# One VectorE step for a complex product, TensorE transposes at the start, and a new order of steps in an attention and convolution kernel

## The chip, the cores and the metric

The kernel runs on one core of a Trainium2 chip. The core has five engines that run side by side and wait for one another through semaphores: TensorE (PE, matrix products), VectorE (DVE), ScalarE (ACT), GpSimd (POOL) and SyncE (SP, which here issues DMAs only). Each engine carries out its own instructions strictly in the order in which they were written. Matrix products land in PSUM, eight banks of 128 x 512 fp32, and are carried ("evicted") from there to SBUF by VectorE or ScalarE; POOL cannot reach PSUM. The metric is the device time of one execution in microseconds (us), the median of several runs; lower is better.

## What is computed

Eight batches, eight heads, 576 positions, 64 features per head. A linear attention with exponential features gives `x`, and a gated long convolution follows, whose convolution is done with a Fourier transform over the 576 positions:

```python
def phi(x):
    proj = np.einsum('bhsd,df->bhsf', x, w_phi)          # 64 -> 128 features
    proj = proj - np.max(np.abs(proj), axis=-1, keepdims=True)
    return np.concatenate([np.exp(proj), np.exp(-proj)], axis=-1)
q_p, k_p = phi(q), phi(k)
kv = np.einsum('bhsf,bhsd->bhfd', k_p, v)
z = np.sum(k_p, axis=2)
x = einsum(q_p, kv) / (einsum(q_p, z) + 1e-6)            # per head, heads side by side: 576 x 512

x1, x2, x3 = split(x @ w_proj, 3)                        # 512 each
X2 = np.fft.rfft(x2, axis=0); H = np.fft.rfft(filter_fft, axis=0)
y = x1 * np.fft.irfft(X2 * H, axis=0) * x3               # X2 * H is the complex product
out = y @ w_out
```

All inputs and the output are fp32 in DRAM; the kernel works in bf16 with fp32 sums.

## The kernel before

**Steps.** Every piece of work is a method of one class, named in a few letters, and most methods issue one instruction or one short group on one engine. They are best read along the path of a batch `b`:

- `load`, `loadh` (L497, L503): POOL issues DMAs that bring a batch of q, k or v (or half of one) to SBUF as bf16. `trh` (L513) is a transposing DMA on SP for half a batch of q or k, from `qn` to `qT`, from `kn` to `kT`.
- `Qn`, `Pk` and `Qnt`, `Pkt` (L535, L528, L542): TensorE projects q and k; `maxq`, `maxk` (VectorE, L600) reduce the absolute maxima from PSUM; `ex`, `exkt`, `exqt` (ScalarE, L584 to L594) write the exponentials. The maxima of q go as two bf16 parts (`mhi`, `mlo`) through a transposing DMA (`trm`, L629, from `mh` to `mT`) back into the q projection (`Pq`, L555), which subtracts them. Those of k scale v: `em` (ScalarE, L634) and `vs` (POOL, L639), one each for both signs and both halves of the heads.
- `KV` (L645) forms kv and z, `KVe` evicts them, `NE` (L669) multiplies by q, `rc` and `xn` (VectorE) divide, and `trx`, `trxt` (L714, L719) are transposing DMAs on SP from `xn` to `xT`.
- `fold`, `foldt` (POOL, L727, L734) form sums and differences of position pairs, `X2` (TensorE, L741) projects them, `X2e` evicts, and `F` (L750, with `dft`, L415) multiplies with DFT tables `fwd`, `fwd5`. `F` has five parts of 128 rows: parts 0 and 1 are a real and an imaginary part, so are 2 and 3, and part 4 has the frequencies left over.
- The complex product with the filter's spectrum: VectorE's `m1` (L756) multiplies each part in PSUM by a table `A`, `Fe` (L753) copies parts 0 to 3 to `C`, POOL's `m2` (L760) multiplies the partner part in `C` by a table `B`, and `m3` (L765) adds.
- `I` (L817) is the inverse transform, even and odd half in two neighbouring banks; `Ie` copies the even half to `es`, `Ip` and `Im` (VectorE, L828) add and subtract. `X1`, `X3` project the gates, `X1e` evicts x1, `tm` multiplies by x3, `ym` (L840) multiplies the gates into the convolution, `O` (L850) projects, `Oe` evicts, and `st` (L860, SP) stores.

A last piece of 64 positions is done apart in most stages (the names with a `t` at the end).

**Set-up.** The DFT tables are made on the chip: POOL counts (`gen_rows`), VectorE and ScalarE form angles and sines into tiles `G` and `g3`, POOL masks some into `G5` (`gen_five`, L367), and two transposing DMAs (`gen_fwd`, `gen_fwd5`, L378) make `fwd` and `fwd5`. POOL also makes `sel` (a one-hot table for the maxima) and `inv`. The filter is loaded (`filt_load`, nine DMAs of 64 KB for each half), folded on POOL (`filt_fold`, L406), transformed (`H`, five matmul groups) and scaled into `A` and `B` (`H_ev`). `warm,n` (L275) issues n matmuls on an idle tile whose product nobody reads: 48 in all, 22 of them at the very start. `late` (L245) closes the set-up tiles and places the tiles of the second half of the kernel in the same memory; it ends with a memset of `eo` on POOL.

**Order.** One string, `PLAN` (L24), lists every step of the kernel in order, with its arguments and, behind `@`, its first PSUM bank; `run` (L874) goes through it word by word. As each engine runs in order, the string sets the order on all five engines and on both DMA queues (SP's and POOL's). Steps of up to three batches are mixed: while attention works on batch b, the second half works on b-1 and stores b-2. A ring (`RING`, L20) gives the number of buffers of each tile; a step takes the buffer `i % n`.

Of the kernel before, what the change touches and what calls it, by code (L numbers as in the profile page):

```python
# [19 lines left out]
RING = {'Ekp': 4, 'Ekm': 4, 'Eqp': 3, 'Eqm': 3, 'vp': 3, 'vm': 3, 'r': 4, 'o': 3, 'kn': 2, 'qn': 2, 'vn': 2, 'kT': 2, 'mk': 2, 'mq': 2, 'mh': 2, 'mT': 2, 'xT': 2, 'xTt': 2, 'KVs': 2, 'Fkp': 2, 'Fkm': 2, 'Fqp': 2, 'Fqm': 2, 'rt': 2, 'xnt': 2, 'xn': 1, 'yT': 2, 'yTp': 2, 'es': 2, 'cv': 2}  # L20
# [16 lines left out]
xn,0,1@0 NE,0,2@0 rc,0,2@0 xn,0,2@0 w_load,proj,2 filt_fold,2 maxkt,1@2 trh,q,1,0 filt_fold,0
filt_fold,1 H,1@4 NE,0,3@0 H_ev,ACT,1@4 rc,0,3@0 rct,0@6 xnt,0,1@6 exkt,m,1@2 xn,0,3@0 H,0@5
trh,q,1,1 xnt,0,0@6 Pk,1,0@2 ex,k,p,1,0@2 trx,0,1 w_load,proj,0 H_ev,DVE,0@5 ex,k,m,1,0@2 gen_inv
trxt,0 Qn,1,0@0 maxq,1,0@0 maxk,1,0@2 trx,0,0 H,2@4 H_ev,ACT,2@4 H,4@6 H_ev,ACT,4@6 warm,4@7  # L40
Pk,1,3@0 Qn,1,1@4 H_fix Qnt,1@6 maxqt,1@6 H,3@2 H_ev,ACT,3@2 X3t,0@3 maxq,1,1@4 load,k,2 em,m,1,0
warm,2@6 Qn,1,3@6 maxq,1,3@6 Qn,1,2@4 ex,k,p,1,3@0 maxq,1,2@4 warm,4@2 Pk,1,2@6 X1t,0@2 maxk,1,2@6
trx,0,3 trx,0,2 X1,0,3@4 late maxk,1,3@0 X1te,ACT,0@2 tmt,0@3 X1,0,2@5 foldt,0,1 mhi,1 w_load,proj,1
em,p,1,0 X1e,DVE,0,2@5 X1,0,0@2 ex,k,p,1,2@6 ex,k,m,1,3@0 X1e,ACT,0,0@2 X1,0,1@3 X1e,ACT,0,1@3
ex,k,m,1,2@6 load,v,1 foldt,0,0 X3,0,2@5 fold,0,0 tm,0,2@5 em,m,1,1 X2,0,4@2 mlo,POOL,1 fold,0,1
X2,0,3@3 X2e,ACT,0,4@2 X2e,DVE,0,3@3 em,p,1,1 X2,0,0@5 X2e,ACT,0,0@5 X3,0,1@2 tm,0,1@2 trm,1
Pq,1,2@6 X1e,DVE,0,3@4 X2,0,1@5 ex,q,p,1,2@6 Pqt,1@2 exqt,p,1@2 X2,0,2@4 trh,k,2,1 X2e,DVE,0,1@5
X2e,DVE,0,2@4 F,0,0@5 X3,0,0@0 exqt,m,1@2 Fe,DVE,0,0@5 tm,0,0@0 ex,q,m,1,2@6 load,q,3 Pq,1,1@2
ex,q,m,1,1@2 ex,q,p,1,1@2 F,0,3@4 m1,0,3@4 m1,0,0@5 F,0,2@0 Fe,DVE,0,2@0 Fe,ACT,0,3@4 F,0,1@1
Fe,DVE,0,1@1 Pq,1,0@6 ex,q,m,1,0@6 load,q,2 load,k,3 vs,m,1,1 vs,p,1,1 KV,1,1@2 KVe,ACT,1,1@2  # L50
vs,m,1,0 m1,0,2@0 vs,p,1,0 trh,k,2,0 KV,1,0@4 KVe,ACT,1,0@4 m2,0,1 m1,0,1@1 m2,0,0 m3,POOL,0,0
NE,1,2@2 rc,1,2@2 xn,1,2@2 m2,0,2 trh,q,2,0 m2,0,3 warm,1@0 NEt,1@4 rct,1@4 xnt,1,1@4 xnt,1,0@4
ex,q,p,1,0@6 Pq,1,3@0 trh,q,2,1 trx,1,2 NE,1,0@6 ex,q,p,1,3@0 ex,q,m,1,3@0 rc,1,0@6 xn,1,0@6
Pk,2,3@2 maxk,2,3@2 F,0,4@4 m1,0,4@4 w_load,out NE,1,1@6 trx,1,0 warm,2@5 NE,1,3@0 rc,1,1@6 xn,1,1@6
ex,k,m,2,3@2 rc,1,3@0 xn,1,3@0 Pk,2,1@4 ex,k,m,2,1@4 m3,POOL,0,1 ex,k,p,2,3@2 trxt,1 Qn,2,0@6
maxq,2,0@6 maxk,2,1@4 I,0,1@0 Ie,0,1@0 Ip,0,1@0 Im,0,1@0 ym,POOL,0,1 I,0,0@6 Ie,0,0@6 Im,0,0@6
Ip,0,0@6 ym,POOL,0,0 ex,k,p,2,1@4 trx,1,3 trx,1,1 Pkt,2@2 exkt,p,2@2 Qn,2,2@0 exkt,m,2@2 maxq,2,2@0
maxkt,2@2 Pk,2,0@4 ex,k,m,2,0@4 Qnt,2@6 maxqt,2@6 Qn,2,1@0 trh,k,3,1 ex,k,p,2,0@4 Qn,2,3@2
maxq,2,1@0 maxq,2,3@2 mhi,2 X3,0,3@6 X1,1,1@7 X1e,ACT,1,1@7 foldt,1,0 maxk,2,0@4 tm,0,3@6 I,0,3@0
Ie,0,3@0 em,m,2,0 Ip,0,3@0 Im,0,3@0 load,v,2 I,0,2@2 Ie,0,2@2 foldt,1,1 X2,1,4@7 Ip,0,2@2 Pk,2,2@4  # L60
fold,1,0 X2,1,0@6 X2e,ACT,1,4@7 X2,1,1@7 mlo,POOL,2 trm,2 em,p,2,0 X1,1,3@0 fold,1,1 ex,k,m,2,2@4
ex,k,p,2,2@4 Im,0,2@2 ym,DVE,0,3 ym,DVE,0,2 X2e,DVE,1,0@6 Pq,2,0@2 ex,q,m,2,0@2 O,0,1@1 Oe,ACT,0,1@1
ex,q,p,2,0@2 maxk,2,2@4 X1,1,2@6 trh,k,3,0 Pq,2,1@4 ex,q,p,2,1@4 X2e,DVE,1,1@7 ex,q,m,2,1@4 load,k,4
X1e,DVE,1,3@0 em,p,2,1 X2,1,2@1 X1e,DVE,1,2@6 st,0,1 Pqt,2@2 exqt,m,2@2 trh,q,3,0 vs,p,2,0 X2,1,3@0
X2e,DVE,1,3@0 vs,m,2,0 X2e,DVE,1,2@1 KV,2,0@6 Pk,3,0@4 KVe,ACT,2,0@6 maxk,3,0@4 F,1,1@0 m1,1,1@0
load,v,3 exqt,p,2@2 em,m,2,1 NE,2,1@6 rc,2,1@6 xn,2,1@6 F,1,4@1 vs,p,2,1 vs,m,2,1 ex,k,p,3,0@4
ex,k,m,3,0@4 Pq,2,2@2 ex,q,p,2,2@2 NE,2,0@6 m1,1,4@1 Pq,2,3@4 ex,q,p,2,3@4 rc,2,0@6 trh,k,4,0
xn,2,0@6 trx,2,0 Fe,DVE,1,1@0 F,1,0@1 m1,1,0@1 KV,2,1@6 m2,1,0 KVe,DVE,2,1@6 F,1,3@0 m1,1,3@0
ex,q,m,2,2@2 NE,2,2@6 rc,2,2@6 Pk,3,1@2 xn,2,2@6 ex,q,m,2,3@4 NE,2,3@4 load,k,5 Fe,ACT,1,0@1 m2,1,1
m3,POOL,1,0 ex,k,p,3,1@2 rc,2,3@4 xn,2,3@4 F,1,2@1 m1,1,2@1 trx,2,1 ex,k,m,3,1@2 trx,2,2  # L70
Fe,ACT,1,2@1 O,0,0@6 Oe,ACT,0,0@6 maxk,3,1@2 Fe,ACT,1,3@0 X3,1,1@7 tm,1,1@7 NEt,2@4 rct,2@4
xnt,2,1@4 X1t,1@1 X1te,ACT,1@1 m2,1,3 xnt,2,0@4 Pk,3,3@2 ex,k,p,3,3@2 maxk,3,3@2 X3,1,3@6 trx,2,3
# [106 lines left out]
class Kernel:  # L179
# [746 lines left out]
```

## Time and profile before

| | us |
|---|---|
| median of 3 runs | 351.43 (348.18 to 353.04) |
| profiled execution, whole time | 351.93 |
| its span, first to last instruction | 350.0 |
| PE busy / PEld busy | 303.4 / 169.5 |
| DVE busy | 257.7 |
| ACT busy | 224.4 |
| POOL busy | 252.3 |
| mean granted TensorE clock | 0.943 of full speed |

The profile is one execution. PE is TensorE's matmuls, PEld its weight loads, which overlap them. A group line reads: line, engine, operation, tile written `<-` tiles read, shape written `<-` shapes read, count, then busy us and mean ns of one, then the idle time of the engine just before them and what ended it. "Idle before" of an engine that doesn't set the time costs nothing. The rows of digits cut the span into 40 slices of 8.75 us: a 9 is a slice that is busy for 90% or more, and in the clock's row a 5 is half speed. A row of the busy times by stretch gives the stretch, its length, the busy time and count of PE, PEld, DVE, ACT and POOL, the granted clock, the DMA engines' mean busy share and GB/s. The timeline and the chain of waits begin with a start time and a duration.

### The profile page before, as it was taken

What the parts mean: (1) busy time and instruction counts of PE and PEld (TensorE: products, weight loads), DVE (VectorE), ACT (ScalarE), POOL (GpSimd) and SP (SyncE); (2) the same over time, 40 slices, a digit from 0 to 9 for tenths busy, and PEclk for the clock granted to TensorE, in tenths of its full rate; (3) what the DMA queues carried; (4) which work ended last, traced back from release to release, by engine and by line L of the source; (5) the groups of instructions that cost most, each with busy time, mean ns of one, the idle gap of its engine ahead of it and who ended that gap; (6) DMA issues with size and microseconds to landing.
All of it is one profiled execution on the core that took longest, in us unless ns stands there. A gap on an engine that the chain in (4) does not pass through costs nothing.

```text
span 350.0 us, 9418 instructions
## 1 busy us (share of the span) xinstructions
PE 303.4 (87%) x3881; PEld 169.5 (48%) x3881; DVE 257.7 (74%) x426; ACT 224.4 (64%) x355; POOL 252.3 (72%) x218
## 2 busy tenths in 40 slices
PE   3560487995979999999998999799999999999982
PEld 1230364443634555556445655454556554665441
DVE  2474048954798789888898898979888987774761
ACT  2746568664667887578477875588567756843531
POOL 8495990889479589898965759456967779678440
PEclk9985559999889999999999999899999999999998
DMA  7999999899979999977495786674695710442236
GB/s 112 154 178 117 173 171 162 137 111 176 148 114 153 128 155 156 185 149 123 83 160 97 98 123 114 106 128 95 137 168 97 109 32 8 101 85 61 53 69 150
DMA packets 83258, 42.68 MB, mean 122 GB/s; under 512 B 63712, under 2 KB 78176, under 8 KB 83216
## 3 DMA queue, kind: packets, MB, share of 16 engines
q1 hardware_dynamic: 68112, 25.25, 45.6%
q0 software_dynamic: 15104, 16.85, 34.0%
q8 instruction: 30, 0.49, 0.6%
q14 instruction: 12, 0.10, 0.1%
HBM read 33.75 MB, written 9.44 MB: 123 GB/s over the span
## 4 chain that ended last, share of the span: by engine, by line
PE 76%; DVE 10%; DMA 8%; ACT 2%; issue 2%; SPq 0%; DVEq 0%; ACTq 0%; POOLq 0%
PE ps L774 17%; PE ps L744 10%; PE ps L427 9%; PE ps L854 8%; PE ps L822 7%; PE ps L656 5%; PE ps L677 4%; DMA mT<-mh 3%; DMA qT<-qn 3%; PE ps L561 3%; DVE yT L842 2%; DVE mq L600 2%; PE ps L540 2%; PE ps L533 2%; PE ps L567 2%
## 5 line engine op out<-in xcount | busy, mean ns | idle before, releaser
L774 PE MATMUL ps<-xT,wproj 128*128 128x512 bf16 x256 | 65.4, 388 | 0.5 <-DVE xnt L708 0.3
L761 POOL TENSOR_TENSOR t<-C,B 128x512 bf16<-128x512 bf16 x32 | 36.4, 1153 | 24.1 <-DVE C L663 21.0
L600 DVE TENSOR_REDUCE mq<-ps 128x8 f32<-128x1024 f32 (+1 forms) x40 | 43.2, 1108 | 9.9 <-PE ps L540 9.5
L600 DVE TENSOR_REDUCE mk<-ps 128x8 f32<-128x1024 f32 (+1 forms) x40 | 43.9, 1110 | 3.6 <-PE ps L533 2.6
L641 POOL TENSOR_TENSOR vp<-vn,vp 128x1152 bf16<-128x1152 bf16 x16 | 34.8, 2177 | 15.9 <-ACT vp L635 15.9
L584 ACT ACTIVATE Eqm<-ps 128x1024 bf16<-128x1024 f32 x32 | 32.6, 1030 | 14.4 <-PE ps L567 13.8
L842 POOL TENSOR_TENSOR yT<-cv,x1s 128x576 bf16<-128x576 f32 x22 | 27.9, 1277 | 18.2 <-DVE cv L831 15.4
L744 PE MATMUL ps<-wproj,eo 128*128 128x512 bf16 x160 | 39.1, 380 | 0.0
L854 PE MATMUL ps<-wout,yT 128*128 128x512 bf16 x144 | 36.2, 380 | 2.0 <-DVE x1s L663 1.0
L427 PE MATMUL ps<-x2n,fwd 128*128 128x512 bf16 x136 | 35.8, 388 | 2.1 <-DVE x1s L663 2.1
L774 PEld LDWEIGHTS <-wproj 128*128 128x128 bf16 x256 | 23.4, 99 | 26.3 <-issue 2.4
L641 POOL TENSOR_TENSOR vm<-vn,vm 128x1152 bf16<-128x1152 bf16 x16 | 34.4, 2151 | 2.2 <-DMA vn<-in_v_dram 1.6
L584 ACT ACTIVATE Ekm<-ps 128x1024 bf16<-128x1024 f32 x32 | 32.7, 1026 | 4.6 <-PE ps L533 3.6
L732 POOL TENSOR_TENSOR eo<-xT 128x1024 bf16<-128x1024 bf16 x16 | 34.0, 2132 | 2.2 <-DMA xT<-xn 2.2
L584 ACT ACTIVATE Eqp<-ps 128x1024 bf16<-128x1024 f32 x32 | 32.5, 1030 | 4.8 <-PE ps L567 2.4
L584 ACT ACTIVATE Ekp<-ps 128x1024 bf16<-128x1024 f32 x32 | 32.7, 1025 | 3.7 <-DVE mk L600 1.8
L661 ACT COPY o<-ps 128x512 f32<-128x512 f32 x29 | 17.0, 587 | 25.6 <-PE ps L854 20.1
L831 DVE TENSOR_TENSOR cv<-es,ps 128x288 f32<-128x288 f32 x64 | 26.1, 447 | 6.6 <-ACT es L826 6.2
L769 POOL TENSOR_TENSOR Y<-Y,t 128x1024 bf16<-128x1024 bf16 x14 | 29.6, 2123 | 1.8 <-DVE Y L757 1.0
L757 DVE TENSOR_TENSOR Y<-ps,A 128x512 bf16<-128x512 f32 x40 | 26.8, 682 | 4.3 <-PE ps L427 4.2
L822 PE MATMUL ps<-inv,Y 128*128 128x288 bf16 x192 | 27.9, 288 | 0.7 <-DVE xn L696 0.4
L811 DVE TENSOR_TENSOR x1s<-ps,x1s 128x512 bf16<-128x512 f32 x32 | 21.8, 686 | 7.6 <-PE ps L774 6.7
(142 smaller groups left out, 635.5 us busy)
## 6 DMA issues: line engine op xcount, KB each, us to landing
out_dram<-o SPq DMA_DIRECT2D x72, 128.0 KB, 2.4
vn<-in_v_dram POOLq DMA_DIRECT2D x8, 576.0 KB, 8.1
kn<-in_k_dram POOLq DMA_DIRECT2D x7, 576.0 KB, 6.7
qn<-in_q_dram POOLq DMA_DIRECT2D x7, 576.0 KB, 8.6
wproj<-in_moe_w_proj_dram POOLq DMA_DIRECT2D x3, 512.0 KB, 6.8
qn<-in_q_dram POOLq DMA_DIRECT2D x2, 288.0 KB, 4.9
kn<-in_k_dram POOLq DMA_DIRECT2D x2, 288.0 KB, 6.5
fl<-in_moe_filter_fft_dram POOLq DMA_DIRECT2D x9, 64.0 KB, 8.6
```

The lines of the kernel that those rows point to most:

```text
L427: self.mm(self.pb(0), l, r, start=(i == 0), stop=(i == len(ks) - 1))
L584: self.nc.scalar.activation(e, self.db(), AF.Exp, bias=0.0, scale=1.0 if g == "p" else -1.0)
L600: self.nc.vector.tensor_reduce(out=out, in_=src, axis=AX.X, op=ALU.max, apply_absolute_value=True)
L641: self.nc.gpsimd.tensor_tensor(out=t[:, :, :, 0:64], in0=self.at("vn", b)[:, 2 * X:2 * X + 2], in1=t[:, :, :, 64:65].to_broadcast([128, 2, ...
L732: self.nc.gpsimd.tensor_tensor(out=o, in0=x[:, :, :, 0, :], in1=x[:, :, :, 1, :], op=op)
L744: self.mm(self.pb(0), eo[:, kt, 128 * c:128 * c + 128], w[:, kt, 512:1024], start=(kt == 0), stop=(kt == 3))
L761: self.nc.gpsimd.tensor_tensor(out=self.at("t2", b)[:, t, :], in0=self.at("C", b)[:, t ^ 1, :], in1=self.at("B")[:, t, :], op=ALU.mult)
L769: e.tensor_tensor(out=Y, in0=Y, in1=self.at("t2", b)[:, s, :], op=ALU.add)
L774: self.mm(self.pb(0), w[:, kt, f0 + 128 * m:f0 + 128 * m + 128], x[:, kt, :], start=(kt == 0), stop=(kt == 3))
L822: self.mm(self.pb(e, 0, 288), Y[:, t, 128 * m:128 * m + 128], inv[:, e, i, :], start=(i == 0), stop=(i == 2))
L842: e.tensor_tensor(out=self.at("yT", b)[:, m, 0:SEQ], in0=self.at("cv", 4 * b + m).rearrange("p j h t -> p (j h t)"), in1=self.at("x1s", b) ...
L854: self.mm(self.pb(0), y[:, kt, 128 * j:128 * j + 128], w[:, kt, :], start=(kt == 0), stop=(kt == 3))
```

## The change

It has three parts.

1. **Complex product.** `Fe`, `m2` and the tiles `C` and `t2` are gone. The filter tables `A` and `B` become one tile `AB` with four pieces for each pair of parts. `m12` reads a part once from PSUM as an operand that is repeated (broadcast) over two pieces of `AB`, and writes both products, 128 x 1024, into a `Y` of four pieces. `m3` adds pieces 0 and 1 to 2 and 3. Part 4 keeps `m1`.
2. **Transposes.** For q and k of batches 0 and 1, for `fwd` and `fwd5`, and for `mT` of batch 0, TensorE transposes 128 x 128 blocks with an identity into PSUM as bf16 (`flip`), up to eight blocks in a bank, and ScalarE or VectorE copies them out (`flop`). The other batches keep the DMA transposes. (`txp`, `txtp` and their copies are defined but not used.)
3. **Order.** `PLAN` is new throughout. `warm` and `hold` do not occur in it. The two halves of `I` are separate steps with a bank each. Buffers of `es`, `cv` and `o` are named in the plan behind `#`. The rings of `Eq` and `v` grow from three to four. The filter loads are all on SP. Twelve evictions of X1 and its tail, seven of O and most of `ym` change their engine, as do ten of `KV`.

```diff
-RING = {... 'Eqp': 3, 'Eqm': 3, 'vp': 3, 'vm': 3, ...}
+RING = {... 'Eqp': 4, 'Eqm': 4, 'vp': 4, 'vm': 4, ...}
+PLACED = ('es', 'cv', 'o')
 PLAN = """
-w_load,phi w_phi zeros loadh,q,0,0 loadh,q,0,1 gen_rows loadh,k,0,0 trh,q,0,0 warm,22@0 Qn,0,0@0
-gen_cols,1 gen_turns,1 gen_cols,0 gen_turns,0 gen_angles,1 Qn,0,1@2 gen_angles,0 maxq,0,0@0
...
+loadh,k,0,0 w_load,phi gen_rows filt_load,SP,1 gen_pads gen_cols,1 loadh,q,0,0 ident gen_cols,0
+gen_turns,1 loadh,q,0,1 loadh,k,0,1 gen_turns,0 gen_angles,1 gen_selidx filt_load,SP,0 zeros
+gen_sin,1 gen_angles,0 gen_five gen_sin,0 tg,0@0 gen_sel tg,2@1 tp,k,0,1@2 tge,DVE,2@1 tp,k,0,0@3
+tpe,ACT,k,0,1@2 tg,1@1 load,k,1 tpe,ACT,k,0,0@3 tp,q,0,1@2 gen_selx tp,q,0,0@4 tpe,ACT,q,0,1@2
+tp,q,0,3@5 tpe,DVE,q,0,0@4 tp,q,0,2@6 w_phi tpe,DVE,q,0,3@5 tpe,ACT,q,0,2@6 tp,k,0,3@7 load,v,0
+tpe,DVE,k,0,3@7 tge,ACT,0@0 Qnt,0@2 Qn,0,0@4 maxqt,0@2 Qn,0,2@6 gen_inv maxq,0,0@4 tp,k,0,2@0
...
+ex,k,p,0,3@4 mlo,DVE,0 Pkt,0@0 filt_fold,2 maxkt,0@0 tpe,ACT,k,1,1@7 Pk,0,2@4 load,q,1 em,p,0,0
+tmp,0@3 maxk,0,2@4 H,0@6 tmpe,ACT,0@3 w_load,proj,0 tpe,ACT,k,1,0@2 exkt,p,0@0 vs,p,0,0 H,3@7
+H_ev,DVE,0@6 em,m,0,0 exkt,m,0@0 em,m,0,1 ex,k,m,0,2@4 Pq,0,1@2 trh,k,2,0 ex,k,p,0,2@4 vs,m,0,0
+H_ev,DVE,3@7 Pqt,0@0 em,p,0,1 ex,q,m,0,1@2 Pq,0,0@4 KV,0,0@6 exqt,m,0@0 vs,p,0,1 ex,q,p,0,1@2
...
@@ H_ev
-            mul(A[:, t, :], acc, s)
-            mul(A[:, t + 1, :], acc, s)
+            mul(AB[:, 0, :], acc, s)
+            mul(AB[:, 3, :], acc, s)
...
-            mul(B[:, t, :], acc, s)
-            mul(B[:, t - 1, :], acc, -s)
+            mul(AB[:, 1, :], acc, s)
+            mul(AB[:, 2, :], acc, -s)
...
+    def pt(self, n):
+        return self.ps[:, self.bank, :].bitcast(BF16)[:, 0:128 * n]
+    def ident(self):
+        idx = self.scr.tile([128, 128], FP32, name="ididx")
+        g = self.nc.gpsimd
+        g.iota(idx, pattern=[[1, 128]], base=0, channel_multiplier=-1,
+               allow_small_or_imprecise_dtypes=True)
+        g.tensor_scalar(out=self.at("idn"), in0=idx, scalar1=0.0, scalar2=None, op0=ALU.is_equal)
+    def flip(self, src, c, n):
+        p, z = self.pt(n), self.at("idn")
+        for i in range(n):
+            self.nc.tensor.transpose(p[:, 128 * i:128 * i + 128],
+                                     src[:, 128 * (c + i):128 * (c + i) + 128], z)
+    def flop(self, eng, dst, n):
+        self.copy(eng, dst, self.pt(n))
+    def tp(self, n, b, i):
+        self.flip(self.at(n + "n", b).rearrange("p v j d -> p (v j d)"), *self.part4(i))
+    def tg(self, i):
+        src = (self.G if i < 2 else self.G5).rearrange("p t x -> p (t x)")
+        self.flip(src, *((0, 8), (8, 4), (0, 5), (5, 5))[i])
+    def tmp(self, b):
+        self.flip(self.at("mh", b).rearrange("p g h x -> p (g h x)"), 0, 1)
...
-    def Fe(self, eng, b, t):
-        self.copy(eng, self.at("C", b)[:, t, :], self.pb(0))
+    def m12(self, b, t):
+        i, h = t // 2, slice(2 * (t % 2), 2 * (t % 2) + 2)
+        self.nc.vector.tensor_tensor(
+            out=self.at("Y", b)[:, i, h, :],
+            in0=self.pb(0).rearrange("p (i x) -> p i x", i=1).to_broadcast([128, 2, 512]),
+            in1=self.at("AB")[:, i, h, :], op=ALU.mult)
     def m1(self, b, t):
-        self.nc.vector.tensor_tensor(out=self.at("Y", b)[:, t, :], in0=self.pb(0), in1=self.at("A")[:, t, :],
+        self.nc.vector.tensor_tensor(out=self.at("Y4", b), in0=self.pb(0), in1=self.at("A4"),
                                      op=ALU.mult)
-    def m2(self, b, t):
-        self.nc.gpsimd.tensor_tensor(out=self.at("t2", b)[:, t, :],
-                                     in0=self.at("C", b)[:, t ^ 1, :],
-                                     in1=self.at("B")[:, t, :], op=ALU.mult)
     def m3(self, eng, b, i):
-        ...
-        e.tensor_tensor(out=Y, in0=Y, in1=self.at("t2", b)[:, s, :], op=ALU.add)
+        Y = self.at("Y", b)[:, i]
+        self.pick(eng).tensor_tensor(out=Y[:, 0:2, :], in0=Y[:, 0:2, :], in1=Y[:, 2:4, :],
+                                     op=ALU.add)
-    def I(self, b, m):
-        Y, inv = self.at("Y", b), self.at("inv")
-        for e in range(2):
-            for i, t in enumerate((2 * e, 2 * e + 1, 4)):
-                self.mm(self.pb(e, 0, 288), Y[:, t, 128 * m:128 * m + 128], inv[:, e, i, :],
-                        start=(i == 0), stop=(i == 2))
+    def I(self, b, m, e):
+        Y, inv, d = self.at("Y", b)[:, e], self.at("inv")[:, e], slice(128 * m, 128 * m + 128)
+        for i, y in enumerate((Y[:, 0, d], Y[:, 1, d], self.at("Y4", b)[:, d])):
+            self.mm(self.pb(0, 0, 288), y, inv[:, i, :], start=(i == 0), stop=(i == 2))
```

From batch 2 on the new order repeats nearly the same sequence of steps for every batch; this is the part from the projection of the maxima of batch 4 to its KV:

```
trh,k,5,1 F,3,0@3 Im,2,2@1#0 em,m,4,0 exkt,m,4@6 Ip,2,2@1#0 F,3,1@0 em,m,4,1 m12,3,2@2
ex,k,m,4,2@4 F,3,4@1 trh,k,6,0 vs,m,4,0 ex,k,p,4,2@4 m12,3,0@3 Pq,4,1@6 em,p,4,1 Pqt,4@4 m12,3,1@0
ex,q,m,4,1@6 F,3,3@2 vs,p,4,1 X3,3,1@3 exqt,m,4@4 m12,3,3@2 ex,q,p,4,1@6 X3,3,0@0 tm,3,1@3
exqt,p,4@4 Pq,4,0@6 vs,m,4,1 m1,3,4@1 KV,4,0@4 ...
```

## The prediction

> **What bounds the kernel now.** I read the page first: busy shares, and the span in 40 slices of 8.75 us.
>
> ```profile
> PE 303.4 (87%) x3881; PEld 169.5 (48%) x3881; DVE 257.7 (74%) x426; ACT 224.4 (64%) x355; POOL 252.3 (72%) x218
> ...
> PE   3560487995979999999998999799999999999982
> ...
> PEclk9985559999889999999999999899999999999998
> ```
>
> TensorE is full from slice 7 on and loses its time in the first seven slices. But 303 us of "busy" counts each matmul's latency. I need its spacing when nothing stands in the way, and take that from the chain of waits, which gives each block with its count.
>
> ```profile
> 5.80 11.05 DMA qT<-qn
> ...
> 26.11 11.31 DMA mT<-mh
> ...
> 70.56 2.59 PE ps L744 x12
> ```
>
> Twelve 512-column matmuls in 2.59 us are 0.216 each. In the same way: 0.122 for 288 columns (L822, twelve in 1.47), 0.016 in KV (L656, 72 in 1.15), 0.031 in NE (L677, 32 in 1.00), some 0.03 for a 128-column projection (starts in the timeline). Counts times spacings: 713 x 0.216 = 154, I 23, KV 18, NE and NEt 20, tails 8, projections 33: 256 us of 350. I also counted the matmuls starting in each stretch at these spacings: 13 us of work in 0 to 60, 47 in 60 to 125, 185 in 125 to 330 (90%), 12 after that. So 94 us are lost: **47 in the head, 18 in the next 65 us, 20 in the long middle, 8 at the end.**
>
> Who holds TensorE in the middle: busy time by stretch (columns: stretch, its length, then PE, PEld, DVE, ACT, POOL with counts, the clock, the DMA share).
>
> ```profile
> 30.00:37.00 7.00, 0.00 (x0) 0.00 (x0) 0.08 (x1) 2.36 (x6) 6.53 (x5) 0.50 1.51 96
> ...
> 45.00:49.00 4.00, 4.00 (x103) 3.58 (x103) 1.33 (x3) 1.57 (x3) 4.00 (x6) 0.50 1.66 202
> ...
> 125.00:300.00 175.00, 170.97 (x2250) 94.42 (x2250) 153.12 (x236) 124.66 (x202) 136.30 (x99) 0.99 0.70 116
> 300.00:330.00 30.00, 30.00 (x351) 17.42 (x344) 20.07 (x40) 15.14 (x27) 21.95 (x17) 1.00 0.30 66
> ```
>
> Where VectorE is 87% busy, TensorE's work fills about 90% of the slots; where VectorE is at 67%, 99%. VectorE's evictions pace TensorE. The first matmuls of KV for batches 0 to 7 start at 41.9, 81.3, 115.9, 147.2, 184.0, 219.8, 259.4 and 298.9: **36.6 us a batch** from batch 2 to 7, and 51 us after the last.
>
> **The product.** Durations by line and shape, and what POOL waited for:
>
> ```profile
> L600 DVE TENSOR_REDUCE mk<-ps 128x8 f32<-128x1024 f32 x32 | 38.6, 1218 | 3.6 <-PE ps L533 2.6 <-ACT Ekp L584 0.9
> ...
> L761 POOL TENSOR_TENSOR t<-C,B 128x512 bf16<-128x512 bf16 x32 | 36.4, 1153 | 24.1 <-DVE C L663 21.0 <-ACT C L661 1.4 <-PE ps L427 1.2
> ...
> L757 DVE TENSOR_TENSOR Y<-ps,A 128x512 bf16<-128x512 f32 x40 | 26.8, 682 | 4.3 <-PE ps L427 4.2
> ...
> L663 DVE CAST C<-ps 128x512 bf16<-128x512 f32 x20 | 13.4, 684 | 4.0 <-PE ps L427 3.9
> ```
>
> Gone are 32 of the 40 multiplies (21.8 us of VectorE), the copies to C (VectorE 13.4, ScalarE 12 x 0.590 = 7.1) and all of m2 (POOL 36.4). New are 32 multiplies of 1024 outputs, whose PSUM operand is read twice; no row shows one. Below: m3 on VectorE, 1024 in 0.694, all from SBUF. Above: ym on VectorE (L842), 576 in 1.432, hence 2.5 for 1024. Nearest is L600, 1024 elements from PSUM in 1.218, in line with 682 ns for 512. I take 1.22: 39.0 us in all, 4 more than what leaves VectorE.
>
> The new order also moves evictions: seven O copies (4.8) and eight X1 copies (5.5) to ScalarE, eight of ten ym (11.5) to POOL, where they cost 8 x 1.277 = 10.2, and ten KV copies (7.0) to VectorE. Back to back, VectorE starts come 0.08 us sooner than durations say (L600 1.13, L757 0.60). At such spacings a batch needs 29.3 us of VectorE before and 28.0 after (15.4 of it maxima, m12 and m1), 31.6 of TensorE both times, some 24 of ScalarE, and of POOL 25 instead of 30.
>
> **The head.** The eight transposing DMAs of batches 0 and 1's q and k go, with the two for the DFT tables and batch 0's mT; the two waits of the chain above (11.05, 11.31) were of that kind. SP gets the nine filter loads that POOL issued (0.5 each). In their place TensorE makes 95 transposes of 128x128, and 21 copies leave PSUM. The nearest row for a transpose is a 128-column projection: 0.03 to 0.06 spacing, 0.22 latency. At 0.06 that is 6 us, beside a TensorE that was idle for 47; at 0.22 it is 21, of which I would expect 10 on the path. The copies hold up to 1024 two-byte elements; by the 256- and 1024-element rows of ScalarE each costs 0.37 to 1.03, some 10 us of ScalarE and 4.5 of VectorE, under the POOL chain that follows.
>
> The Trainium skill, "TensorE: Matmul & The Clock Gate", Part 4, puts a transpose at about 275 ns inside a kernel and says that the full clock doesn't engage for it. By that, 95 x 0.275 = 26 us (an estimate); no row here shows it.
>
> The 48 fillers on idle operands go (15.4 us of latency time). The rows above show what they kept up: despite them the clock stood at 0.50 from 30 to 49. So I charge nothing for their loss before batch 0, and up to 3 us after it. Part 1 of that page has the clock halved after an idle window of about 3.4 us and restored by as long a busy one; by that rule all 9 us of TensorE's early work would take 18, again inside its idle time.
>
> What is late next is **POOL's queue**, in its new order. VectorE no longer begins with the wait for w_phi (4.94 us), so the sines come some 2.5 us sooner, at 11. Then POOL: mask products (L373, L375) 5.1, one-hot 1.5, load of k 0.8, sel 2.1, load of v 0.8, inv 3.5, load of k 0.8: 26. The six filter sums, 6 x 1.268 less overlap: 33. Two loads, 1.6; two scalings of v (L641), 4.3: **KV of batch 0 at 39**, 3 sooner than now. TensorE has H ahead of the q projections, so they also wait for the filter sums at 33.
>
> From there the gap closes further, since now POOL stands still in front of the folds:
>
> ```profile
> 51.52 0.79 POOL L498 DMA_DIRECT2D kn<-in_k_dram  x1
> 62.52 0.31 POOL L261 MEMSET eo<- 128x256 bf16 x1 [10.21 <-issue]
> 62.80 0.42 POOL L738 TENSOR_TENSOR eo<-xTt 128x128 bf16<-128x128 bf16 x1
> ...
> 65.11 2.14 POOL L732 TENSOR_TENSOR eo<-xT 128x1024 bf16<-128x1024 bf16 x1
> ```
>
> The memset (late) follows the last readers of the set-up tiles, the H matmuls. In the new order H,4 comes right after NE of batch 0, at about 50; xn is done at 51, its transposes land 3.7 us later, a fold takes 2.1: **first X2 matmul near 57, against 70.6 now.**
>
> **The sum.** From 57 on TensorE has 242 us of spacing (its 262 less some 20 in the head). Idle: 8 at the end as now; in the middle 200 us of work at 93%, that is 34.0 a batch, 15; 5 while batch 1 fills. 57 + 242 + 28 = 327. The profiled execution is 351.9 for a span of 350.0, so **329 us**. It stands 0.5 us over the median of 351.43 (348.18 to 353.04), which is what the ratio is taken against. About 2% is what this kernel's measurement can tell from no change. I take 93%, between 90 and 99%, because VectorE is lighter by 4% and the folds and m3 no longer wait for 4.6 us of m2 a batch.
>
> **The rivals.**
> - *The order, not the load, sets the period.* By the list of steps, 32.5 us of TensorE's work lie between two KV starts now; the same efficiency over 31.6 makes 35.6 and 340 in all, the upper end of my own case. At 36.5 to 37.5, seven batches cost 2.5 to 3.5 us more each: 346 to 354. For it: both orders are written out, TensorE runs in order, and each attention step needs two of eight banks. If m12 costs 2.5 us, VectorE needs 33 us a batch, at 90% of a period 37, and it comes to the same, near 350. Against: 300 to 330 above, where lighter VectorE meant a full TensorE.
> - *The transposes of xn arrive late: slower.* SP issues two transposes of q for the next batch just before the four of xn; a pair holds SP for up to 6.47 us (timeline at 5.8). By my count X1 of the new batch needs xT about 3 us after it lands. If queueing adds over 7.5 us to the 2.5 us median, every batch loses 4.5, seven of them 31: 360. Against: the DMA share is 0.70 in the middle, and the early transposes are gone from the crowded stretch.
> - *The product's shorter path lets TensorE run at 97 to 99%,* as in 300 to 330: 311 to 318.
> - *The change doesn't do what it says*: TensorE's transposes take longer than the DMAs, by the 0.22 or worse, 10 to 14 us later in the head: 339 to 343.
>
> **Chances.** 0.60 for the forecast (320 to 340), 0.12 for the fast case, 0.06 for slow transposes on TensorE, 0.14 for the order (346 to 354), 0.08 for slower. Range 311 to 347: it leaves out the slow case and the upper part of the order. Faster by over 2% (under 344.4): 0.78; same 0.14; slower 0.08.
>
> **What would show it.** m12 near 1.22 us; KV of batch 0 near 39 with POOL without gaps before it; X2 from 57; KV starts 33 to 35 apart; VectorE under 90% of the middle; about 50 us behind the last KV. I am wrong if POOL idles in the head (then another engine sets it), or if TensorE's matmuls wait for xT or for bank releases by more than 15 us in the middle.

## The result, and the profile after

The changed kernel takes 331.32 us (median of four runs, 329.35 to 332.42) against 352.24 (348.18 to 353.55) for the kernel before: **0.944 of the time, 95% interval 0.933 to 0.954**. The prediction was 329. Run once more beside other kernels it took 327.55, a ratio of 0.941 [0.935, 0.947]. The profiled execution took 332.42 us with a span of 330.6. All ratios here compare undisturbed executions alone, so they can differ by up to 1% from the quotient of the medians beside them.

Busy times, and rows of the span in 40 slices, of the page after; a slice is now 8.27 us:

```profile
PE 283.4 (86%) x3893; PEld 171.6 (52%) x3928; DVE 248.2 (75%) x398; ACT 226.1 (68%) x364; POOL 223.7 (68%) x186
...
PE   0463777898789999999997999999999989999982
...
PEclk9995779999999999999999899999999999999998
```

TensorE starts later than before (the first slice is empty, the fillers are gone), but from the fifth slice to the last but one none is under 7, where the row before has a 4 and a 5. POOL has lost 28.6 us of busy time, VectorE 9.5.

Two stretches of the middle (stretch, length, then PE, PEld, DVE, ACT, POOL with counts, the clock, the DMA share, GB/s):

```profile
125.00:280.00 155.00, 148.65 (x2069) 88.09 (x2089) 131.10 (x197) 115.84 (x189) 112.06 (x80) 0.99 0.78 127
280.00:310.00 30.00, 29.84 (x354) 17.87 (x350) 20.17 (x38) 13.65 (x24) 17.90 (x12) 1.00 0.29 66
```

VectorE is busy for 85% of the middle. KV starts at 37.3, 73.0, 107.5, 140.8, 175.1, 211.6, 245.4 and 279.0: from batch 2 to 7 **34.3 us a batch** against 36.6 before, and 51.6 behind the last KV against 51. So of the 19.4 us between the two spans (350.0 and 330.6) 8.4 are gained up to KV of batch 2 (115.9 before, 107.5 now) and 11.5 from there to KV of batch 7 (183.0 and 171.5).

POOL's timeline in the head (start, duration, engine, line, work, and in brackets the wait before it):

```profile
25.90 4.92 POOL L429 TENSOR_TENSOR fe<-fl,fl 128x512 bf16<-128x512 f32 x4
30.79 2.58 POOL L431 TENSOR_TENSOR fe<-fl,fl 32x512 bf16<-32x512 f32 x2
33.33 0.79 POOL L518 DMA_DIRECT2D qn<-in_q_dram  x1
34.11 0.75 POOL L487 DMA_DIRECT2D wproj<-in_moe_w_proj_dram  x1
34.92 2.14 POOL L714 TENSOR_TENSOR vp<-vn,vp 128x1152 bf16<-128x1152 bf16 x1
...
52.78 0.30 POOL L277 MEMSET eo<- 128x256 bf16 x1 [8.65 <-PE ps L446]
...
56.63 4.21 POOL L808 TENSOR_TENSOR eo<-xT 128x1024 bf16<-128x1024 bf16 x2 [2.11 <-DMA xT<-xn]
```

From the filter sums to the first scaling POOL has no gap; then it waits 8.65 us for the last H matmuls, and 2.11 for the transposes of xn. The first X2 matmul starts at 58.8, against 70.4 before.

The two groups of the complex product (mean ns of one, then the idle time before them):

```profile
L831 DVE TENSOR_TENSOR Y<-ps,AB 128x1024 bf16<-128x1024 f32 x32 | 36.9, 1212 | 2.9 <-PE ps L446 2.9
...
L842 POOL TENSOR_TENSOR Y<-Y 128x1024 bf16<-128x1024 bf16 x15 | 32.0, 2152 | 4.6 <-DVE Y L831 4.6
```

### The profile page after: what moved, and what is told of

It is laid out like the page before. It is cut to its first block, busy times and chain, and to the rows that moved or that the text cites. A ratio compares the mean times of both kernels' runs of the same rounds, so it can differ in the third digit from the quotient of the medians.

```text
span 330.6 us, 9406 instructions
## 1 busy us (share of the span) xinstructions
PE 283.4 (86%) x3893; PEld 171.6 (52%) x3928; DVE 248.2 (75%) x398; ACT 226.1 (68%) x364; POOL 223.7 (68%) x186
## 4 chain that ended last, share of the span: by engine, by line
PE 57%; POOL 15%; DMA 11%; DVE 6%; issue 5%; ACT 4%; SPq 0%; POOLq 0%; ACTq 0%; DVEq 0%
PE ps L848 13%; PE ps L820 8%; PE ps L446 8%; PE ps L926 7%; PE ps L729 5%; PE ps L895 4%; PE ps L750 4%; DMA qT<-qn 3%; DMA xT<-xn 3%; POOL vp L714 3%; POOL vm L714 3%; DMA xTt<-xnt 2%; PE ps L634 2%; PE ps L640 2%; DMA mT<-mh 2%
## 5 line engine op out<-in xcount | busy, mean ns | idle before, releaser
L914 POOL TENSOR_TENSOR yT<-cv,x1s 128x576 bf16<-128x576 f32 x30 | 37.9, 1277 | 51.4 <-DVE cv L903 29.5
L848 PE MATMUL ps<-xT,wproj 128*128 128x512 bf16 x244 | 61.8, 380 | 2.1 <-DMA xT<-xn 1.3
L714 POOL TENSOR_TENSOR vp<-vn,vp 128x1152 bf16<-128x1152 bf16 x16 | 34.3, 2145 | 8.7 <-ACT vp L708 8.6
L820 PE MATMUL ps<-wproj,eo 128*128 128x512 bf16 x157 | 37.7, 380 | 2.5 <-POOL eo L814 1.5
L831 DVE TENSOR_TENSOR Y<-ps,AB 128x1024 bf16<-128x1024 f32 x32 | 36.9, 1212 | 2.9 <-PE ps L446 2.9
L808 POOL TENSOR_TENSOR eo<-xT 128x1024 bf16<-128x1024 bf16 x16 | 33.8, 2133 | 7.0 <-DMA xT<-xn 6.9
L734 ACT COPY o<-ps 128x512 f32<-128x512 f32 x36 | 21.0, 593 | 25.4 <-PE ps L926 21.7
L842 POOL TENSOR_TENSOR Y<-Y 128x1024 bf16<-128x1024 bf16 x15 | 32.0, 2152 | 4.6 <-DVE Y L831 4.6
L714 POOL TENSOR_TENSOR vm<-vn,vm 128x1152 bf16<-128x1152 bf16 x16 | 34.3, 2144 | 0.0
L734 ACT CAST x1s<-ps 128x512 bf16<-128x512 f32 (+1 forms) x37 | 19.9, 538 | 18.9 <-PE ps L848 8.2
L446 PE MATMUL ps<-x2n,fwd 128*128 128x512 bf16 x134 | 31.8, 379 | 0.1
L895 PE MATMUL ps<-inv,Y 128*128 128x288 bf16 x192 | 31.1, 286 | 0.0
L898 ACT COPY es<-ps 128x288 f32<-128x288 f32 x32 | 12.0, 401 | 24.2 <-PE ps L895 13.1
```

Of the source, the lines that this page charges most:

```text
L446: self.mm(self.pb(0), l, r, start=(i == 0), stop=(i == len(ks) - 1))
L714: self.nc.gpsimd.tensor_tensor(out=t[:, :, :, 0:64], in0=self.at("vn", b)[:, 2 * X:2 * X + 2], in1=t[:, :, :, 64:65].to_broadcast([128, 2, ...
L734: self.nc.scalar.copy(dst, src)
L808: self.pick(eng).tensor_tensor(out=o, in0=x[:, :, :, 0, :], in1=x[:, :, :, 1, :], op=op)
L820: self.mm(self.pb(0), eo[:, kt, 128 * c:128 * c + 128], w[:, kt, 512:1024], start=(kt == 0), stop=(kt == 3))
L831: self.nc.vector.tensor_tensor(out=self.at("Y", b)[:, i, h, :], in0=self.pb(0).rearrange("p (i x) -> p i x", i=1).to_broadcast([128, 2, 512]),
```

## The experiments

A "period" is the mean distance of the first exponentials of k's tail (`exkt`) from batch 2 to 7; the kernel before has no such fixed place for them, so for it the starts of KV are taken. The changed kernel's period by this measure is 34.3 in its first profile and 34.2 in its second. Ratios are to the kernel before on the same chip.

### The product alone, in the old order

```diff
 the kernel before, with AB, Y of four pieces, m12 and m3 of the changed kernel;
 PLAN as before, but for
-Fe,DVE,0,0@2 m1,0,0@2 ... m2,0,0
+m12,0,0@2
```

> The kernel before with the complex product alone changed: m12 where m1 stood for parts 0 to 3, Fe and m2 gone, the old order of all other steps. POOL loses 36 us, ScalarE 7, VectorE changes by about +4. Theory (VectorE's evictions and the order pace TensorE, POOL's product does not): 346 to 354 us, at most 5 below the kernel before, first X2 matmul still at 70, about 36 us from KV to KV. Rival (POOL's long product was what held the old order back, so the product is the source of the gain): 332 to 342 us, KV starts 34 to 35 apart.

Measured: 351.26 us, ratio 1.004 [0.999, 1.008]. **Nothing.** POOL's busy time fell from 252.3 to 216.6, and the first m3 stands at 84.0 against 84.2, behind a wait of 2.81 us for VectorE's products, the second at 86.9 against 89.3. In 125 to 280 VectorE is busy for 139.9 of 155 us against 136.5 before: the old order keeps `ym` and the X1 and O copies on VectorE, and VectorE's total grows from 257.7 to 264.3. What is taken from POOL doesn't shorten the whole there.

### The old product, in the new order

```diff
 the changed kernel, with
     def m12(self, b, t):
+        copy the PSUM part to Y[i, partner];  Y[i, own] = PSUM part * AB      (VectorE, 512 each)
     def m3(self, eng, b, i):
+        for h in 0, 1:  Y[i, 1 + h] = Y[i, 1 + h] * AB[i, 1 + h]              (POOL, 512 each)
         Y[i, 0:2] = Y[i, 0:2] + Y[i, 2:4]
```

> The kernel after with the old way of the product: for each of parts 0 to 3 VectorE copies the part out of PSUM and multiplies it once, and POOL multiplies the copies just ahead of m3; all else in the new order. VectorE gets some 0.3 us more a batch, POOL 4.6 more (25 to 30 of a period of 34). Theory (the product's worth in the new order is POOL's free time ahead of m3, ym and the folds): 335 to 343 us, head unchanged, KV starts 35 to 36 apart. Rival 1 (POOL's share is hidden): 330 to 334. Rival 2 (the product is the main source of the gain): 345 or more.

Measured: 354.64 us, 1.009 [1.002, 1.016]: slightly slower than the kernel before, and by the ratios some 24 us above the changed kernel (0.941 in its second run). The head keeps its gain (first fold at 55.2), but the period is 37.8, and the stretch behind the last KV 59.3 us instead of 51.6. So what the product is worth depends on the order: nothing in the old one, over 20 us in the new one (with the old multiplies at this place of POOL's queue; earlier ones were not tried). Two rows say where. First, what TensorE's matmuls waited for in 125 to 280 (total, times, longest), then POOL's timeline for one batch:

```profile
PE ps L897 <- POOL Y L844: 12.1, 7, 2.5
```

```profile
144.62 2.26 POOL L842 TENSOR_TENSOR Y<-Y,AB 128x512 bf16<-128x512 bf16 x2
146.96 2.12 POOL L844 TENSOR_TENSOR Y<-Y 128x1024 bf16<-128x1024 bf16 x1
149.05 2.27 POOL L842 TENSOR_TENSOR Y<-Y,AB 128x512 bf16<-128x512 bf16 x2
151.39 2.12 POOL L844 TENSOR_TENSOR Y<-Y 128x1024 bf16<-128x1024 bf16 x1
159.84 1.28 POOL L916 TENSOR_TENSOR yT<-cv,x1s 128x576 bf16<-128x576 f32 x1 [6.34 <-PE ps L928]
```

The inverse transform (L897) waits for the sums (L844), and each sum now has 2.3 us of POOL ahead of it. In the changed kernel the view of the same stretch names no wait for m3 at all. Yet POOL stands idle 6.34 us right behind: it has the time, only not there. Whether it was the place or something else in the old product (its VectorE copies, one more step between engines) is the question of the next pair.

### POOL's work ahead of the sum, and behind it

Both are the changed kernel with extra POOL multiplies into a tile that nobody reads.

```diff
 e9:  ahead of each m3
+dum: W[h] = Y[i, 1 + h] * AB[i, 1 + h]  for h in 0, 1      (POOL, 128 x 512, 30 in all)
 m3,POOL,b,i
 e10: behind the second m3 of a batch
 m3,POOL,b,1
+dum: W[h] = AB[i, 1 + h] * AB[i, 1 + h] for h in 0, 1, i in 0, 1   (28 in all)
```

> The changed kernel, with two extra POOL multiplies of 128 x 512 ahead of each m3, where the old m2 stood; they read Y and AB and write a tile that nobody reads, so TensorE, VectorE and ScalarE have no instruction more. 30 of them at about 1.15 us are 35 us of POOL. Theory (POOL's place in the chain from m12 over m3 to the inverse transform and to the next scalings is what made the old product slow in the new order): m3 and all that follows on POOL comes 4.6 us later in every batch, the period goes from 34 to about 37.5, and the time to 345 to 356. Rival (it was VectorE's and ScalarE's copies, or the extra step from engine to engine): POOL has 30% to spare, the time stays within 330 to 337.

> The changed kernel with the same POOL work (28 multiplies of 128 x 512, some 32 us), but behind the second m3 of a batch, where POOL next waits for the even and odd halves of the inverse transform. Theory (place): part of the 4.6 us a batch falls into POOL's own waiting; the time is 331 to 342, clearly less than with the work ahead of m3. Rival (POOL's load as such, or the SBUF traffic of POOL beside VectorE): the same time as with the work ahead of m3, within 2%.

Measured: ahead of m3 351.46 us, 1.002 [0.997, 1.008], with a period of 37.4 in a profiled execution of 352.07; behind it 327.56, 0.942 [0.937, 0.946], the same as the changed kernel beside them (327.55). By the ratios **the place alone is worth about 21 us.** No instruction of VectorE, ScalarE or TensorE differs between the three. TensorE's wait in 125 to 280 with the work ahead is that of the old product above (then the group of the extra multiplies):

```profile
PE ps L903 <- POOL Y L850: 10.9, 6, 2.4
```

```profile
L846 POOL TENSOR_TENSOR W<-Y,AB 128x512 bf16<-128x512 bf16 x30 | 34.4, 1164 | 3.5 <-DVE Y L833 3.4
```

And with the work behind m3, POOL's groups of the gates and of the extra multiplies, with the gates of the changed kernel ahead of them:

```profile
L914 POOL TENSOR_TENSOR yT<-cv,x1s 128x576 bf16<-128x576 f32 x30 | 37.9, 1277 | 51.4 <-DVE cv L903 29.5
```

```profile
L922 POOL TENSOR_TENSOR yT<-cv,x1s 128x576 bf16<-128x576 f32 x30 | 37.9, 1275 | 20.1 <-DVE cv L911 9.9 <-PE ps L934 7.4 <-DVE x1s L893 2.8
...
L846 POOL TENSOR_TENSOR W<-AB 128x512 bf16<-128x512 bf16 x28 | 28.2, 1031 | 0.0
```

POOL's idle time before `ym` is 20.1 us; it is 51.4 in the changed kernel. The 28.2 us of extra work lie in that gap and cost nothing. So POOL's load, up to these 28 us more, was not the matter; what counts is how long the chain through m12, m3 and the inverse transform takes.

### VectorE loaded

```diff
     def m12(self, b, t):
+        for o in (W, Y[:, i, h, :]):           (W: a tile that nobody reads)
             vector.tensor_tensor(out=o, PSUM part repeated * AB)
```

> The kernel after with every m12 done twice, the first time into a tile that nobody reads: four times 1.13 us, 4.5 more on VectorE in a batch (28.0 to 32.5 back to back), and each product 1.1 us later. Theory (VectorE paces TensorE in the middle; it idles some 3 us of each period, part of which this fills): KV starts 36 to 38 apart, 343 to 360 us. Rival (TensorE or the transposes' landing set the period and VectorE has room): under 337 us.

Measured: 358.0 us, 1.021 [1.012, 1.030], by the ratios some 28 us above the changed kernel; the period is 37.8 (from 101.2 to 290.3 in five batches). An m12 more costs 1.21 us, 4.8 a batch, and 3.5 of these come back in the period.

```profile
PE ps L849 <- DVE Y L833: 10.8, 8, 1.5
```

In the middle, X1 and X3 (L849) wait for banks that the two multiplies hold. VectorE's time at this place sets the period, as does POOL's step between m12 and the inverse transform: both lie on one chain. Whether the same VectorE time at another place would cost as much was not tried, so that VectorE's load as such paces the changed kernel is not shown.

### The early transposes by DMA again

```diff
 the changed kernel, PLAN with
-tp,k,0,1@2 tpe,ACT,k,0,1@2 tp,k,0,0@3 tpe,ACT,k,0,0@3 ... tg,0@0 tge,ACT,0@0 ... tmp,0@3 tmpe,ACT,0@3
+trh,k,0,0 ... gen_fwd gen_fwd5 ... trm,0
```

> The kernel after with all of TensorE's transposes given back to transposing DMAs on SP (q and k of batches 0 and 1, the two tables, mT of batch 0) at the place of the first of them; the order is otherwise the new one. Theory (in the new head POOL's queue comes last, up to the filter sums at 33 and the scalings of v from 35, so slower transposes are mostly covered): KV of batch 0 at 38 to 43, 333 to 341 us. Rival (the transposes themselves are the head's gain): KV of batch 0 at 45 or later and 343 us or more.

Measured: 346.64 us, 0.990 [0.986, 0.994]. Against the changed kernel's 0.941 that is **17 us for the transposes**, all in the head: POOL's first scaling of v starts at 48.1 (34.9 in the changed kernel), the first fold at 77.0 (56.6), the first X2 matmul at 79.1 (58.8), and the period stays at 33.6. I had expected POOL's queue to hide most of it, and that fell for a reason POOL's timeline shows:

```profile
23.11 1.99 POOL L408 TENSOR_SCALAR inv<-g,msk 128x288 bf16<-128x288 bf16 x2
38.25 0.80 POOL L513 DMA_DIRECT2D kn<-in_k_dram  x1 [13.15 <-DMA kT<-kn]
39.08 1.28 POOL L424 TENSOR_TENSOR fe<-fl,fl 128x512 bf16<-128x512 f32 x1
```

The load of batch 2's k stands ahead of the filter sums in POOL's queue, and there are two buffers of `kn`: it has to wait until batch 0's k is transposed. TensorE's transposes free the buffer early; the DMAs do so 13 us later, and POOL stands still with all that is behind the load. In the kernel after, POOL has no such wait (its timeline above). Later, at 76.96, the first fold waits 9.56 us more for the transposes of xn. TensorE also ran at half speed in this kernel until 58.8 us (last section); how much of the 17 us that is was not tried.

### The filter sums on VectorE

```diff
     def filt_fold(self, i):
-        g = self.nc.gpsimd
+        g = self.nc.vector
 PLAN: the three filt_fold behind maxk,0,2@4; H,0 and H,3 with their H_ev behind KVe,DVE,0,1
```

> The kernel after with the six filter sums moved from POOL (7.5 us) to VectorE behind the maxima of batch 0, and the first two H behind the first KV; all else as in the kernel after. Theory (POOL's queue sets the head: sums to 33.4, two loads, scalings of v from 34.9): the scalings start near 29, the first KV 3 to 4 us sooner than 37.3, the first X2 matmul 3 to 6 sooner than 58.8, 325 to 328 us. Rival (another engine is right behind POOL, or the later stages take the time back): 330 us or more.

Measured: 331.61 us, 0.950 [0.942, 0.958], no gain. The scalings of v start 5.4 us sooner (29.5 against 34.9), but POOL then waits for the same things:

```profile
39.24 0.81 POOL L487 DMA_DIRECT2D wproj<-in_moe_w_proj_dram  x1
54.42 0.31 POOL L277 MEMSET eo<- 128x256 bf16 x1 [14.37 <-PE ps L446]
...
56.59 4.21 POOL L808 TENSOR_TENSOR eo<-xT 128x1024 bf16<-128x1024 bf16 x2 [0.24 <-DMA xT<-xn]
```

The wait before the memset grows from 8.65 to 14.37, and the fold stands at 56.6 as before. The H matmuls, and xn behind them, end no sooner when POOL is early. Part of this is the edit's own, since VectorE does the sums and H moves behind KV.

### The fillers back

```diff
 PLAN of the changed kernel, 23 of the 48 fillers
+warm,10@0
 tg,0@0 ...
+warm,4@6
 Pkt,0@0 ...
+warm,5@7
 H,0@6 ...
+warm,4@2
 tp,q,1,1@2 ...
```

> The kernel after with 23 filler matmuls put back where its TensorE idles in the head: ten before the first transposes, four before Pkt of batch 0, five before the first H, four after the first KV. Theory (nothing is lost by leaving the fillers out, since TensorE waits in the head for POOL and VectorE at either clock): 330 to 333 us, the first KV within 1 us of 37.3. Rival (the half clock from 24 to 36 costs time): 3 us or more faster, first X2 matmul before 57.

Measured: 327.46 us, 0.937 [0.931, 0.943]; the changed kernel again, on another chip:

> The changed kernel, unaltered, on the chip of the three others, so that they can be compared with it directly: 327 to 332 us, 0.935 to 0.950 of the kernel before. The kernel with fillers had 0.937; if this one comes out at 0.945 or more, the fillers are worth 2 to 4 us, if at 0.94 or less, nothing.

Measured: 327.55 us, 0.941 [0.935, 0.947]. The intervals overlap, so no gain is shown. The clock did follow (rows of the kernel after and then of the one with fillers, for 24 to 36 us):

```profile
24.00:36.00 12.00, 6.20 (x45) 3.01 (x47) 9.19 (x11) 8.76 (x17) 11.84 (x12) 0.50 0.78 119
```

```profile
24.00:36.00 12.00, 7.54 (x63) 3.85 (x64) 9.56 (x11) 9.15 (x17) 11.84 (x12) 0.86 0.78 121
```

Clock 0.86 instead of 0.50 in those 12 us brings nothing forward: POOL's first scaling starts at 34.9 in both, the first fold at 56.6 without fillers and 58.9 with them. POOL is busy for 11.84 of the 12 us in both rows, and the scalings are POOL's own next work.

### The transposes of xn later

```diff
 PLAN, every batch (both kernels); the second one with the filter sums on VectorE too
-trx,b,2 ... trx,b,3 ... trxt,b
+trxt,b trx,b,2 ... trx,b,3
```

> The kernel after with one step moved for every batch: the transposing DMA of the tail (from xnt to xTt) before the third of the four of xn on SP instead of behind them and a store. In the kernel after POOL stood 10.0 us in front of the tail's folds waiting for it. Theory (this is the part of the rival of late transposes that came true: foldt holds X2, and with it Pkt and the maxima behind it, 1 to 2 us a batch): 320 to 327 us. Rival (X2 and VectorE are held by something else at the same time): 329 us or more.

> The moves of the two kernels before it together: filter sums on VectorE with H behind the first KV, and the tail's transpose earlier. If both theories hold the gains add, since one is in the head and the other in the middle: 315 to 323 us. If only one holds, its own value.

Measured: 344.52 us, 0.979 [0.967, 0.990], and with the filter sums on VectorE 342.71, 0.981 [0.973, 0.989]: by the ratios 13 to 14 us more than the changed kernel (0.941), and for the second 11 more than the kernel with the filter sums alone (0.950), lost by one transpose of 1.2 us that goes first. The second kernel is read here. Its second pair of transposes lands later than in the changed kernel (second profile) by 8.6 us in batch 0, 13.7 in batch 1, and then by 13.8, 14.4, 16.5, 15.6, 16.2 and 14.1. **All of this kernel's loss is in the first two batches.** (The first kernel's profile, of an execution of 344.76 us, is 10.0 us late at KV of batch 2 and 14.8 at KV of batch 7, so there it is most of the loss and not all.) POOL's timeline shows the first one, of this kernel and then of the changed one:

```profile
54.98 0.31 POOL L277 MEMSET eo<- 128x256 bf16 x1 [14.63 <-PE ps L446]
55.44 0.74 POOL L487 DMA_DIRECT2D wproj<-in_moe_w_proj_dram  x1
56.17 0.75 POOL L518 DMA_DIRECT2D vn<-in_v_dram  x1
64.00 4.21 POOL L808 TENSOR_TENSOR eo<-xT 128x1024 bf16<-128x1024 bf16 x2 [7.08 <-issue]
```

```profile
51.84 0.74 POOL L487 DMA_DIRECT2D wproj<-in_moe_w_proj_dram  x1
52.57 0.75 POOL L518 DMA_DIRECT2D vn<-in_v_dram  x1
55.37 4.21 POOL L808 TENSOR_TENSOR eo<-xT 128x1024 bf16<-128x1024 bf16 x2 [2.06 <-DMA xT<-xn]
```

In the changed kernel the last transpose of xn is issued at 51.3, half a microsecond ahead of the loads of `wproj` and `vn` (512 and 576 KB), and lands after 4.0 us. Here it is issued at 55.7, 0.3 us behind the first of these loads and 0.5 ahead of the second, and lands after 8.2; the fold starts 0.1 us behind that. Of the 8.6 us of batch 0, 4.4 are thus the later issue (the kernel with the filter sums alone has 2.8 of them too) and 4.2 the slower landing. With the filter sums alone the last transpose is issued 0.7 us ahead of the first load and lands after 2.4. And in the changed kernel it is the tail's transpose, issued at 52.6 behind both loads, that lands after 8.2:

```profile
xTt<-xnt SPq DMA_TRANSPOSE x1, 8.2
```

From batch 2 on the same swap leaves the period where it was (33.8, with the filter sums alone 33.8).

### SP's order the other way

```diff
 PLAN with the fillers, every batch from 1 on
-trh,k,b+2,0 ... trh,q,b+1,1 ... trh,q,b+1,0 trx,b,... trxt,b
+trh,q,b+1,1 trh,q,b+1,0 ... trx,b,... trxt,b trh,k,b+2,0
```

> The changed kernel with the 23 groups of filler matmuls of the earlier run, and SP's order changed: the two transposes of the next batch's q are issued earlier, at the place of the first half of the k of the batch after that, which moves behind the transposes of xn and xnt. Theory (the transposes of xn wait on SP behind those of q, and every batch waits for xT): xT lands 1 to 3 us sooner in each batch, the period falls to 31.5 to 33, the time to 311 to 322. Rival (VectorE paces the middle, so an earlier xT is waited for by nobody): 325 to 330, as with the fillers alone.

Measured: 369.45 us, 1.062 [1.056, 1.069]. This run doesn't test what it was made for. `qT` is a single buffer; the new place lies between the projections `Pq` of a batch, so that most of them are formed from the next batch's q in this kernel, and TensorE has to wait for that load and its transposes:

```profile
PE ps L634 <- DMA qT<-qn: 33.0, 5, 8.6
```

What it does show is that waits in TensorE's own queue are paid in full and more: 33.0 us of waiting go with 42 us of time over the changed kernel. The mean granted clock fell with them, from 0.969 to 0.911; how much of the other 9 us that is, isn't shown. Whether an earlier xT would help the changed kernel is open.

## Why the prediction was right

The time came out 2.3 us above the forecast, and the two halves of the sum, up to the first X2 matmul and from there, within 2 us each. That it fits so closely is in part luck: two sizes that the runs found, 21 us for POOL's place ahead of m3 and 17 for the transposes, stand in the sum as no terms of their own; they are inside a head of 57 us and a share of 93% that was chosen from between 90 and 99. By its steps:

- **m12 at 1.22 us**, taken from the reduction of the same shape: 1.212. The second reading of the PSUM operand costs nothing beyond the 1024 outputs.
- **KV of batch 0 at 39, first X2 near 57**: 37.3 and 58.8. The filter sums end at 33.4 (33 predicted), the first scaling starts at 34.9 (35), the memset stands at 52.8 (about 50). "What is late next is POOL's queue" holds up to the scalings. Behind that, POOL waits for the H matmuls and xn, as the prediction's next sentence said, and the run with the filter sums on VectorE shows that POOL's 7.5 us there are not the only limit.
- **34.0 us a batch**: 34.3, which is 31.6 over 0.92. From the first X2 matmul to the end of the span are 271.8 us, where the prediction had 270.
- **The reason given for 93%** was two things in one number: "VectorE is lighter by 4% and the folds and m3 no longer wait for 4.6 us of m2 a batch". The step was right but mis-sized inside: the second half alone is worth about 21 us in this order (work ahead of m3 against work behind it), 3.2 a batch by the periods. The first has the weight of the run with m12 twice, 3.5 us of period for 4.8 us of VectorE, so 1.3 us less of VectorE at that place would be some 0.9 a batch (an estimate from that run). They don't simply add: the product without the order brings nothing.
- **POOL "25 instead of 30"** stood in the prediction as a load. That was the wrong way to count it: 28 us more of POOL behind m3 cost nothing, 34 us ahead of it 21.
- **The signs of being wrong.** POOL does idle in the head, 8.65 and 2.11 us, but behind KV of batch 0, where the prediction itself has it stand in front of the folds. TensorE's waits from 125 to 280 that the view names come to 4.9 us, far from 15, and none is for xT or for VectorE; the two largest:

```profile
PE ps L729 <- issue: 2.9, 2, 2.3
PE ps L820 <- POOL eo L814: 0.9, 1, 0.9
```

  So the view doesn't tell what most of the missing 8% of the middle is, and "VectorE's evictions pace TensorE" stays argued.
- **The transposes on TensorE** were put at 0.06 us, 6 us in all, up to 0.22. The timeline of TensorE has both a slower and a faster stretch:

```profile
15.57 1.97 PE L553 MATMUL ps<-idn,qn 128*128 128x128 bf16 x18
...
19.23 0.44 PE L553 MATMUL ps<-idn,kn 128*128 128x128 bf16 x5 [0.23 <-ACT fwd L734]
```

  Eighteen in 1.97 us, with 0.31 for the last one's latency, are 0.10 apart; five in 0.44 with a latency of 0.22 are 0.055. With 61 of the 95 at the slow spacing they take about 8 us in all (an estimate from these two spacings), in time in which TensorE had been idle. "TensorE: Matmul & The Clock Gate", Part 4, of the Trainium skill has 275 ns for one: as a duration that agrees (265, 282 and 289 ns in the mean for the three kinds), but as room taken in the queue, 26 us, it doesn't. What they are worth, 17 us, is over the 13.6 that the prediction found in the head altogether (70.6 to 57): it didn't see that with the transposes back on DMA the new order would stop POOL, at a load that waits for `kn`.
- **The fillers** at nothing before batch 0 and up to 3 us after it: no difference is shown.
- **Rivals.** "The order sets the period" (346 to 354) was wrong for the change, but is what the product alone does: 351. "The transposes of xn arrive late" was said to cost 4.5 us in every batch if they came 7.5 later; in the one kernel read for it they cost 11 to 14 us, all in the first two batches, where the last of them came behind a load. TensorE at 97 to 99% and slow transposes didn't come.

What stays open is what the order is worth by itself: taken back one at a time, the product costs 24 us and the transposes 17, more than the whole gain of 20, and neither the transposes alone in the old order nor the new order without both was run. Open is also what ends the old order's period. VectorE's 90% of the middle fits, but no run changed that alone. That the middle of the changed kernel could be filled better isn't shown either: every change of its order that was run either made it slower or made no difference.

## What to carry to other kernels

Ask of an engine with time to spare not how busy it is but what is queued on it ahead of the step that the full engine waits for: here 34 us of POOL work cost 21 us ahead of one add, and 28 us of it nothing behind that add. A change of the arithmetic and a change of the order (here with the transposes) can each be worth nothing and together 6%, so try each alone before crediting either. And follow a queue past its computing: POOL's filter sums stood behind a load that waited for a buffer, and a transpose issued 0.3 us behind a load instead of 0.5 ahead of it took twice as long to land.

## What the runs showed of the hardware that was not expected

- A transpose on SP that POOL's loads preceded by less than a microsecond landed late: after 8.2 us when it was issued 0.3 us behind a load of 512 KB, and after 8.2 behind two loads, against 4.0 and 2.4 when it was issued 0.5 and 0.7 us ahead of them. No run moved the loads alone.
- TensorE's full clock came after nothing but transposes. In the changed kernel its first 5 us of work, from 12.24 on, are transposes, 0.10 us apart. The trace's table of clock changes begins at 17.23 us, with full speed, and the next transposes there, and those at 19.2, stand 0.055 apart. At 24.4, where the row says 0.52, they are 0.10 apart again. Part 4 of the Trainium skill's page named above says that the full clock doesn't engage for transposes; these spacings are against that, if it means transposes such as these, which the trace calls MATMUL.
- A stretch ahead of a trace's first clock change is no measured clock, though the rows print 1.00 for it: in the changed kernel 12 to 17 us, where the spacing is that of half speed. With the early transposes on DMA, TensorE was all but idle until 36 us, and the first change stands at 58.76. The rows say 1.00 from 24 to 60, but sixteen matmuls of KV took 0.66 us before it and 0.43 after:

```profile
54.99 0.66 PE L724 MATMUL ps<-vm,Ekm 64*128 64x65 bf16 x16
...
59.05 0.43 PE L724 MATMUL ps<-vm,Ekm 64*128 64x65 bf16 x16
```

  By these spacings TensorE ran at half speed there until about 58.8 us.
